# Second weight group of the first layer converted after the attention's scores, first group earlier

## The chip, the cores and the metric

The kernel runs on one core of one Trainium2 chip. Its time is device microseconds (us) of that core, from one launch with all inputs in device memory. Engines are named as in the profile: PE multiplies matrices (PEld is its loading of the stationary operand), DVE is the vector engine, ACT the scalar engine, POOL the GpSimd engine, SP the engine whose queue issues the DMAs. Each engine works through its own instructions in the order in which the program lists them, and waits on semaphores for what others make.

## The reference

```python
q_assign = argmax(norm(q) @ norm(centroids).T); k_assign likewise      # 2 x 8 heads, 768 tokens, 64 wide
scores = where(q_assign == k_assign, q @ k.T / sqrt(64), -1e9)
attn_out = softmax(scores) @ v
x  = attn_out as 1536 x 512
h  = x @ moe_w_in                       # 512 x 2048
x2 = (h * sigmoid(1.702 * h)) @ moe_w_out   # 2048 x 512
h2 = x2 @ moe2_w_in                     # 512 x 1024
out = layernorm(h2 * softmax(h2)) * g_ln @ moe2_w_out
```

Inputs are fp32. The weights `w_in` and `w_out` are read as pairs of 32-bit words (`raw`), turned into fp32 by integer operations, and split into two fp16 halves (high and low), so that each product is three fp16 matmuls.

## The kernel before

**Attention.** 16 heads in 8 pairs. A head has nine units (parts of its 768 x 768 scores), so there are 144 units, and units are also the clock by which due times are given. For each unit PE makes a first product whose row maxima DVE takes (line 927, then the reduction in line 938), then the scores (lines 982 and 983, a PSUM bank `st`), ACT takes the exponential (line 991), ACT or DVE casts it to fp16 (line 996, `ph`), POOL or DVE subtracts to get the low half (line 1000, "the rest"), and PE multiplies by the values (lines 1015, 1018, 1019, `av`). For some units, and for every odd one from unit 120 on, the exponential stays in its PSUM bank: then DVE makes the rest, and the bank is free for a later score only when that is done.

**First weights.** `w_in` (object `w1`) has 16 chunks of 128 x 512 in four groups. A chunk is loaded (line 183), then *narrowed* by three DVE operations (lines 194, 199, 203, all reading and writing `reg`), then squared with a row sum on ACT (line 213). When the four chunks of a group are squared, PE adds up the sums (`bound`, line 139, tile `tot` or `ex`), DVE makes a power of two of it (lines 145 to 153), and each chunk is split: high on ACT (line 234), low on DVE (line 237). A load needs a raw buffer (two in the attention, a third in the first layer), which comes free when an earlier chunk is narrowed. `w_out` (object `wo`) goes the same way, in one group of 16 chunks.

**First layer.** 48 steps of 12 matmuls (line 1187, tile `hps`), of which steps 1 to 8 need the first group, 9 to 16 the second, and so on to the fourth; the last 16 use all. Each step is followed by the gate (line 1194) and the high half (line 1197) on ACT, and by the low half on DVE (line 1205) or POOL (lines 1202, 1203). Then come `w_out`'s products (lines 1352 and 1364) and the second block.

**What sets the order.** Everything up to the 48 steps is a list of tasks with a cost per engine, a due time and the tasks that it waits for. `Plan.order` places them one after another: on each engine it takes, of the tasks that can start within 0.1 us of the earliest, the one with the smallest due time. The kernel is then written out in that order, so each engine's queue is fixed by it; the chip itself waits only for data and buffers. `tail=0` marks the tasks of the attention whose end opens the first layer's buffers. `weights(w, c, due)` adds the tasks of group c. With `begun=True` only loads, narrowing and squares are added (as `tail=0`), and `later` keeps the group for `scaled`, which adds bound, power, high and low when the first layer is set up, in `rest_of_layer`.

Before the change the first group is due over units 20 to 122, and the second group's loads, narrowing and squares over units 122 to 144; its bound and splits wait for the scores. Third and fourth group are added in `rest_of_layer`.

Of the kernel before, what the change touches and what calls it, by code (L numbers as in the profile page):

```python
# [21 lines left out]
def kernel(  # L22
# [29 lines left out]
    NH = B * H  # L52
# [16 lines left out]
    E1 = -10  # L69
    E2 = 0  # L70
    E3 = 0
    NG = 2
    WDUE = 0
    XDUE = 60
    VDUE = 3
# [22 lines left out]
    LN = 512.0  # L98
    WLATE = 6
    WAHEAD2 = 6  # L100
    W0, W1 = 20, 122

    const = ctx.enter_context(tc.tile_pool(name="const", bufs=1))
    wp = ctx.enter_context(tc.tile_pool(name="wp", bufs=1))
# [198 lines left out]
    w1 = Weight(0, w_in, "w1", reg1, group=w_in.shape[0] // P)  # L303
# [121 lines left out]
    NU = 9  # L425
# [247 lines left out]
    def late(x):  # L673

        return [T["PC", 0, 0, 1]] if x else []
# [112 lines left out]
    def bound(t, sums):  # L788

        t["tile"] = bank(t)  # L790
        power_sum(t["tile"], sums)
# [62 lines left out]

    narrows = []

    def weights(w, c, due, after=None, then=None, scores=(), begun=False):


        sums, parts = [], {}  # L860
        kw = dict(tail=2 if after else 0)
        n = CV + bool(scores)
        open_, kw = kw, dict(tail=0) if begun else kw
        chunks = range(c * w.group, (c + 1) * w.group)

        def step(i, k):
            if k == 0:
                parts[i] = w.narrow(i)
            next(parts[i])

        def powers(a):
            w.powers[c] = power_from(a["tile"][:, 0:w.group])
            if then:
                then()

        for i in chunks:
            d = due(i)
            prev = add(
                dict(SP=(0.47, 1.46)), d, lambda t, i=i: w.load(i),
                after=[narrows[-n] if len(narrows) >= n else None] + list(scores or late(True)), **kw  # L880
            )
            for k, x in enumerate((0.34, 0.6, 0.6)):
                prev = add(
                    dict(DVE=x), d + 3 + k, lambda t, i=i, k=k: step(i, k),
                    after=[prev] + (after if after and w is wo else []), shared=True, **kw
                )
            narrows.append(prev)
            sums.append(add(dict(ACT=0.61), d + 6, lambda t, i=i: w.square(i), after=[prev], **kw))
        kw = open_
        if begun:  # L890
            later.append((w, c, sums, powers, due))
            return
        scaled(w, c, sums, powers, due, after, kw)

    later = []

    def scaled(w, c, sums, powers, due, after, kw):
        chunks = range(c * w.group, (c + 1) * w.group)
        d = due(chunks[-1])
        a = add(  # L900
            dict(PE=0.1), NH * NU if after else d + 8, lambda t: bound(t, w.squares(c)), after=sums + (after or []),
            take="acc" if after else "ex", **kw
        )
        a = add(dict(DVE=0.9), NH * NU if after else d + 8, lambda t, a=a: powers(a), after=[a], frees=a, **kw)
        for i in chunks[0:WLATE if w is wo else w.group]:
            b = add(
                dict(ACT=0.61), d + 12, lambda t, i=i: w.high(i),
                after=[a, at("WL", w, i - 2)], **kw
            )
            T["WL", w, i] = add(dict(DVE=0.66), d + 13, lambda t, i=i: w.low(i), after=[b], shared=True, **kw)  # L910
# [352 lines left out]
    def rest_of_layer():  # L1263

        scores = [t for t in plan.tasks if t["tail"] == 0]
        result = [t for t in plan.tasks if t["tail"] <= 1]
        steps = blocks + [(2, m) for m in range(NF)]
        n0 = NH * NU + 100
        for x in later:
            scaled(*x[:4], lambda i: n0 - 70, scores, dict(tail=2))  # L1270
        for c in range(NG, w1.n // w1.group):
            weights(w1, c, lambda i: n0 + WAHEAD + 4 * i - w1.n, after=scores)
        weights(wo, 0, lambda i: n0 + WOD + 4 * i, after=result, then=even, scores=scores)
        for k, (n, m) in enumerate(steps):
            x, d = Hidden(n, m, k % 2), n0 + 2 * k
            a = add(
                dict(PE=1.92), d, lambda t, x=x: x.products(),
                after=[T["WL", w1, w1.ready(m) - 1]] + (result if n == 2 else scores), take="acc", tail=2,
            )
            T["HP", k] = a  # L1280
            b = add(
                dict(ACT=0.46), d, lambda t, x=x: x.gate(), after=[a] + [at("HL", k - 6)] * x.out,
                frees=a if x.out else None, tail=2,
            )
            c = add(dict(ACT=0.5), d, lambda t, x=x: x.high(), after=[b], tail=2)
            T["HL", k] = add(
                dict(POOL=1.45) if x.out else dict(DVE=0.5), d, lambda t, x=x: x.low(), after=[c],
                frees=None if x.out else a, tail=2,
            )
# [3 lines left out]
    peaks_of(0)  # L1293
    values()
    weights(w1, 0, lambda i: W0 + (W1 - W0) * i / w1.group)
    weights(w1, 1, lambda i: W1 + (NH * NU - W1) * (i - w1.group) / w1.group, begun=True)
    for p in range(NH // 2):
        if p:
            operands_of(p)
# [283 lines left out]
```

## Time and profile before

| | us |
|---|---|
| three runs | 618.36 median, 617.84 to 619.15 |
| the profiled execution | 617.67 |
| its span in the trace | 615.9 |
| PE busy in the span | 600.4 (97%) |
| DVE, ACT, POOL busy | 430.3, 391.9, 272.7 |

The profiled execution is 1.77 us longer than its span (the launch around it) and 0.69 us below the median of the three runs. In the profile a group or an instruction is named by engine, line, operation and tiles; behind an instruction stands in brackets how long its engine had been idle, and what ended that. Rows of windows give the busy time of each engine in a stretch, with the instruction count in brackets, and PEclk is the share of the full TensorE clock (2.4 GHz) that was granted.

### The profile page before, as it was taken

What the parts mean: (1) busy time and instruction counts of PE and PEld (TensorE: products, weight loads), DVE (VectorE), ACT (ScalarE), POOL (GpSimd) and SP (SyncE); (2) the same over time, 40 slices, a digit from 0 to 9 for tenths busy, and PEclk for the clock granted to TensorE, in tenths of its full rate; (3) what the DMA queues carried; (4) which work ended last, traced back from release to release, by engine and by line L of the source; (5) the groups of instructions that cost most, each with busy time, mean ns of one, the idle gap of its engine ahead of it and who ended that gap; (6) DMA issues with size and microseconds to landing.
All of it is one profiled execution on the core that took longest, in us unless ns stands there. A gap on an engine that the chain in (4) does not pass through costs nothing. (4 is left out here: it accounts for less than half of the span.)

```text
span 615.9 us, 12736 instructions
## 1 busy us (share of the span) xinstructions
PE 600.4 (97%) x4873; PEld 393.8 (64%) x4873; DVE 430.3 (70%) x967; ACT 391.9 (64%) x768; POOL 272.7 (44%) x247
## 2 busy tenths in 40 slices
PE   7999999999999979999999999999999999999997
PEld 6787788888788755666656666666665554444444
DVE  6999998899899997798985043075966455654542
ACT  4498899898899877878787055435335334544442
POOL 7259987776678762356643019600000112331320
PEclk9999999999999997999999999999999999999999
DMA  8898989968885156445630002051410112434241
GB/s 188 209 234 173 193 165 174 180 153 162 174 173 120 29 129 173 127 137 181 196 103 0 1 1 71 0 171 36 136 35 2 36 34 52 100 55 103 52 102 52
DMA packets 78772, 67.91 MB, mean 110 GB/s; under 512 B 61636, under 2 KB 64536, under 8 KB 78712
## 3 DMA queue, kind: packets, MB, share of 16 engines
q1 hardware_dynamic: 78712, 67.11, 46.2%
q8 instruction: 38, 0.62, 0.4%
q14 instruction: 22, 0.18, 0.1%
HBM read 34.64 MB, written 3.15 MB: 61 GB/s over the span
## 5 line engine op out<-in xcount | busy, mean ns | idle before, releaser
L1000 POOL TENSOR_TENSOR ph<-p,ph 128x512 f16<-128x512 f32 x108 | 129.9, 1219 | 53.7 <-ACT ph L996 27.9
L1187 PE MATMUL hps<-xT,reg 128*128 128x384 f16 x768 | 128.2, 330 | 0.0
L1187 PEld LDWEIGHTS <-reg 128*128 128x128 f16 x768 | 76.1, 100 | 50.7 <-issue 2.7
L938 DVE TENSOR_REDUCE nma<-sm 128x1 f32<-128x512 f32 (+1 forms) x144 | 96.6, 679 | 6.5 <-PE sm L927 5.8
L1364 PE MATMUL yps<-g,reg 128*128 128x384 f16 x576 | 94.6, 326 | 0.0
L1364 PEld LDWEIGHTS <-reg 128*128 128x128 f16 x576 | 56.4, 98 | 37.0
L1454 POOL TENSOR_TENSOR rs<-va,mhalf 128x1 f32<-128x1 f32 x12 | 6.6, 550 | 150.9 <-DVE va L1452 150.9
L1202 POOL TENSOR_SCALAR g<-g,scl 128x384 f32<-128x384 f32 x40 | 33.5, 838 | 88.8 <-ACT g L1197 81.2
L982 PE MATMUL st<-OP 128*128 128x256 f32 (+1 forms) x191 | 69.9, 377 | 2.5 <-DVE ph L1000 1.1
L991 ACT ACTIVATE p<-st 128x512 f32<-128x512 f32 x107 | 63.4, 597 | 9.2 <-PE st L983 8.2
L1413 PE MATMUL h<-reg,xT 128*128 128x512 f16 x288 | 64.1, 379 | 0.0
L1019 PE MATMUL av<-vh,ph 128*128 128x65 f16 x576 | 61.3, 195 | 1.7 <-POOL ph L1000 1.4
L983 PE MATMUL st<-OP 97*128 97x512 f32 (+3 forms) x191 | 62.8, 340 | 0.0
L1015 PE MATMUL av<-vh,ph 128*128 128x65 f16 x576 | 62.1, 194 | 0.0
L1018 PE MATMUL av<-vh,ph 128*128 128x64 f16 x576 | 61.4, 193 | 0.0
L1015 PEld LDWEIGHTS <-ph 128*128 128x128 f16 x576 | 52.7, 99 | 12.6 <-issue 11.2
L927 PE MATMUL sm<-OP 80*128 80x512 f32 x192 | 58.1, 359 | 1.1 <-DMA OP<-oht 0.7
L996 ACT CAST ph<-p 128x512 f16<-128x512 f32 x94 | 57.1, 616 | 1.2 <-PE av L1019 0.7
L1019 PEld LDWEIGHTS <-ph 128*128 128x128 f16 x576 | 53.6, 97 | 2.2 <-POOL ph L1000 1.9
L1018 PEld LDWEIGHTS <-ph 128*128 128x128 f16 x576 | 53.7, 97 | 0.1
L1489 PEld LDWEIGHTS <-g 128*128 128x128 f16 x312 | 30.4, 98 | 32.1 <-DMA g<-g 0.7
L1413 PEld LDWEIGHTS <-xT 128*128 128x128 f16 x288 | 28.2, 98 | 33.4
(204 smaller groups left out, 1132.7 us busy)
## 6 DMA issues: line engine op xcount, KB each, us to landing
OP<-hl SPq DMA_DIRECT2D x48, 384.0 KB, 4.8
raw<-in_moe_w_in_dram SPq DMA_DIRECT2D x24, 512.0 KB, 3.8
raw<-in_moe_w_out_dram SPq DMA_DIRECT2D x24, 512.0 KB, 3.4
xT<-in_v_dram SPq DMA_DIRECT2D x8, 384.0 KB, 4.5
out_dram<-ob SPq DMA_DIRECT2D x11, 256.0 KB, 2.3
raw<-in_k_dram SPq DMA_DIRECT2D x12, 192.0 KB
raw<-in_q_dram SPq DMA_DIRECT2D x12, 192.0 KB, 5.9
OP<-oht SPq DMA_DIRECT2D x30, 48.0 KB, 2.7
```

The lines of the kernel that those rows point to most:

```text
L927: nc.tensor.matmul(t["tile"][:, at], Q1[0:KM, j * P:(j + 1) * P], K1[0:KM, cs], start=True, stop=True)
L938: nc.vector.tensor_reduce(out=out, in_=src, op=ALU.max, axis=AX.X, negate=True)
L982: nc.tensor.matmul(t["tile"][:, at], K2[:, ks], Q2[:, cs], start=True, stop=False)
L983: nc.tensor.matmul(t["tile"][:, at], K1[0:n, ks], Q1[0:n, cs], start=False, stop=True)
L991: nc.scalar.activation(p32s[u, m], t["tile"], AF.Exp, scale=SCALE)
L1000: e.tensor_tensor(out=phs[u, m][:, 1], in0=p32s.pop((u, m)), in1=phs[u, m][:, 0], op=ALU.subtract)
L1015: nc.tensor.matmul(av[:, i, :], ph[:, 0, qs], vh[:, u, kt, D:], start=(m == 0 and i == 0), stop=False,)
L1018: nc.tensor.matmul(av[:, i, 0:D], ph[:, 0, qs], vh[:, u, kt, 0:D], start=False, stop=False)
L1019: nc.tensor.matmul(av[:, i, :], ph[:, 1, qs], vh[:, u, kt, D:], start=False, stop=(m == NU - 1 and kt == NJ - 1 and i == NJ - 1),)
L1187: nc.tensor.matmul(self.ps, w1.at(c, m, e), xT[:, x, c, n * TB:(n + 1) * TB], start=(c == 0 and e == x), stop=(c == ND - 1 and e == 1),)
L1364: nc.tensor.matmul(yps, wo.at(f, c, e), lp["g", n][:, x, f, :], start=(f == 0 and e == x), stop=(f == NF - 1 and e == 1),)
L1413: nc.tensor.matmul(h, xT[:, x, c, t * P:(t + 1) * P], w2.half(i * ND + c, e), start=(c == 0 and e == x), stop=(c == ND - 1 and x == 1),)
```

## The change

The first group's due times now run over units 20 to 80. The second group is no longer begun in the attention: all its tasks are added in `rest_of_layer`, like those of the third and the fourth, with due times behind the scores and its bound after them. `begun`, `later` and `scaled` go.

```diff
-    NG = 2
+    NG = 1
-    W0, W1 = 20, 122
+    W0, W1 = 20, 80
...
-    def weights(w, c, due, after=None, then=None, scores=(), begun=False):
+    def weights(w, c, due, after=None, then=None, scores=()):
...
         kw = dict(tail=2 if after else 0)
         n = CV + bool(scores)
-        open_, kw = kw, dict(tail=0) if begun else kw
...
-        kw = open_
-        if begun:
-            later.append((w, c, sums, powers, due))
-            return
-        scaled(w, c, sums, powers, due, after, kw)
...
-        for x in later:
-            scaled(*x[:4], lambda i: n0 - 70, scores, dict(tail=2))
         for c in range(NG, w1.n // w1.group):
             weights(w1, c, lambda i: n0 + WAHEAD + 4 * i - w1.n, after=scores)
...
     weights(w1, 0, lambda i: W0 + (W1 - W0) * i / w1.group)
-    weights(w1, 1, lambda i: W1 + (NH * NU - W1) * (i - w1.group) / w1.group, begun=True)
```

The plan reorders all engines. Lines of the changed kernel behind the removed ones are 12 to 15 lower (938 is 926, 991 is 979, 996 is 984, 1000 is 988, 1187 is 1175, 1205 is 1193).

DVE at the end of the attention, before: `ph` and `st` are the rests and casts of the last units, `reg1` with raw_3930 and raw_4415 the second group's second and third chunk.

```order
L1000 TENSOR_TENSOR ph_4461<-st_4385,ph_4461 128x512
L203 SCALAR_TENSOR_TENSOR reg1_105<-raw_3930,reg1_105 128x512
L1000 TENSOR_TENSOR ph_4478<-st_4427,ph_4478 128x512
L194 TENSOR_SCALAR reg1_105<-raw_4415 128x512
L1045 CAST xh_4528<-xs_4273 128x768
L199 SCALAR_TENSOR_TENSOR reg1_105<-raw_4415,reg1_105 128x512
L1030 TENSOR_SCALAR ri_4539<-av_4348 128x6
L1032 RECIPROCAL ri_4539<-ri_4539 128x6
L1000 TENSOR_TENSOR ph_4537<-st_4473,ph_4537 128x512
```

The same units now; raw_3240 is the second group's first chunk.

```order
L988 TENSOR_TENSOR ph_4431<-st_4385,ph_4431 128x512
L984 CAST ph_4468<-st_4428 128x512
L988 TENSOR_TENSOR ph_4468<-st_4428,ph_4468 128x512
L199 SCALAR_TENSOR_TENSOR reg1_105<-raw_3240,reg1_105 128x512
L988 TENSOR_TENSOR ph_4510<-st_4470,ph_4510 128x512
L1018 TENSOR_SCALAR ri_4538<-av_4348 128x6
L1020 RECIPROCAL ri_4538<-ri_4538 128x6
L203 SCALAR_TENSOR_TENSOR reg1_105<-raw_3240,reg1_105 128x512
```

Between the last reduction and the last rest DVE had ten narrowing operations (lines 194 to 203); it now has three, and one more stands earlier. The other eight of the second group come behind the last rest.

ACT at the same place, before: the third and the fourth square stand on either side of the last unit's exponential (`st_4594`).

```order
L991 ACTIVATE st_4582<-st_4582 128x512
L991 ACTIVATE p32_4599<-st_4588 128x512
L213 ACTIVATE junk_104,wss_101<-reg1_105 128x512
L991 ACTIVATE st_4594<-st_4594 128x512
L996 CAST ph_4637<-p32_4599 128x512
L213 ACTIVATE junk_104,wss_101<-reg1_105 128x512
```

And now:

```order
L984 CAST ph_4609<-p32_4568 128x512
L979 ACTIVATE p32_4618<-st_4580 128x512
L213 ACTIVATE junk_104,wss_101<-reg1_105 128x512
L979 ACTIVATE st_4613<-st_4613 128x512
L984 CAST ph_4651<-st_4613 128x512
L213 ACTIVATE junk_104,wss_101<-reg1_105 128x512 x2
L1182 ACT_TABLE_LOAD
```

One square, the group's first, stands ahead of the last exponential in place of three; the second and third follow the last cast, and the fourth comes in the first layer.

PE where the first layer begins, before: the last value matmuls, the second group's bound, the first step.

```order
L1019 LDWEIGHTS ph
L1019 MATMUL av<-vh,ph 128x65
L139 MATMUL tot<-wss,ones 128x4
L1187 LDWEIGHTS reg_105
L1187 MATMUL hps<-xT,reg_105 128x384
```

And now, where the first step begins (the last unit's twelve value matmuls follow it), and where the bound stands, behind the fifth step:

```order
L1007 LDWEIGHTS ph
L1007 MATMUL av<-vh,ph 128x65
L1175 LDWEIGHTS reg_105
L1175 MATMUL hps<-xT,reg_105 128x384
L1175 LDWEIGHTS reg_105
```

```order
L1175 LDWEIGHTS reg_105
L1175 MATMUL hps<-xT,reg_105 128x384
L139 MATMUL tot<-wss,ones 128x4
L1175 LDWEIGHTS reg_105
L1175 MATMUL hps<-xT,reg_105 128x384
```

The bounds of third group, fourth group and `w_out` stood behind steps 9, 16 and 39; they now stand behind steps 13, 21 and 44. The first group's bound, which stood among the attention's last third on PE, stands near its middle, and six casts of the attention's units have gone from DVE to ACT.

## Rows read from the trace of the kernel before

**Rows 1.** The page's first part: busy time, share, instructions.

```profile
PE 600.4 (97%) x4873; PEld 393.8 (64%) x4873; DVE 430.3 (70%) x967; ACT 391.9 (64%) x768; POOL 272.7 (44%) x247
```

**Rows 2.** Windows by stage: length, PE, PEld, DVE, ACT, POOL, PEclk, DMA, GB/s.

```profile
80.00:150.00 70.00, 70.00 (x901) 59.80 (x898) 63.67 (x133) 62.85 (x120) 52.53 (x44) 1.00 0.88 175
150.00:205.00 55.00, 54.19 (x723) 45.04 (x722) 49.60 (x106) 49.78 (x96) 42.58 (x35) 1.00 0.64 134
205.00:232.00 27.00, 21.51 (x343) 16.54 (x339) 25.98 (x45) 20.63 (x43) 15.53 (x13) 0.98 0.39 89
240.00:310.00 70.00, 70.00 (x435) 42.37 (x433) 61.97 (x113) 56.95 (x124) 36.99 (x35) 1.00 0.52 164
```

**Rows 3.** Waits from 205 to 233 us: in total, times, longest.

```profile
ACT junk L213 <- DVE reg L203: 5.3, 4, 3.1
...
PE tot L139 <- ACT junk L213: 1.6, 1, 1.6
PE av L1019 <- POOL ph L1000: 1.4, 2, 0.8
...
PE st L982 <- DVE ph L1000: 1.1, 2, 0.6
...
PE st L982 <- ACT p L991: 0.9, 1, 0.9
```

**Rows 4.** Timeline of DVE, ACT and PE at the attention's end.

```profile
218.44 1.66 DVE L203 SCALAR_TENSOR_TENSOR reg<-raw,reg 128x512 uint32<-128x512 uint32 x1
...
220.13 0.63 ACT L213 ACTIVATE junk<-reg 128x512 bf16<-128x512 f32 x1 [0.90 <-DVE reg L203]
...
220.76 0.58 ACT L991 ACTIVATE st<-st 128x512 f32<-128x512 f32 x1
...
222.41 0.38 PE L982 MATMUL st<-OP 128*128 128x256 f32 x1 [0.86 <-ACT p L991]
...
232.04 0.59 PE L139 MATMUL tot<-wss,ones 128*128 128x4 f32 x2 [1.59 <-ACT junk L213]
```

**Rows 5.** Groups of 205 to 232 us: count, busy, mean ns, idle before.

```profile
L203 DVE SCALAR_TENSOR_TENSOR reg<-raw,reg 128x512 uint32<-128x512 uint32 x4 | 5.2, 1294 | 0.0
...
L199 DVE SCALAR_TENSOR_TENSOR reg<-raw,reg 128x512 uint32<-128x512 uint32 x5 | 4.1, 824 | 0.0
...
L194 DVE TENSOR_SCALAR reg<-raw 128x512 uint32<-128x512 uint32 x5 | 2.7, 536 | 0.0
L213 ACT ACTIVATE junk<-reg 128x512 bf16<-128x512 f32 x4 | 2.5, 631 | 5.3 <-DVE reg L203 5.3
```

**Rows 6.** Windows of line 1187 on PE: length, PE, PEclk, DMA, GB/s.

```profile
230.00:235.00 5.00, 2.51 (x8) 0.58 0.36 107
235.00:240.00 5.00, 5.00 (x24) 0.74 0.98 217
240.00:245.00 5.00, 5.00 (x33) 1.00 0.57 175
```

**Rows 7.** Groups of 80 to 205 us on DVE.

```profile
L996 DVE CAST ph<-p 128x512 f16<-128x512 f32 x11 | 5.1, 468 | 0.8 <-ACT p L991 0.8
...
L199 DVE SCALAR_TENSOR_TENSOR reg<-raw,reg 128x512 uint32<-128x512 uint32 x4 | 3.9, 966 | 0.1
...
L237 DVE SCALAR_TENSOR_TENSOR reg<-reg,scl 128x512 f16<-128x512 f32 x4 | 3.1, 796 | 0.0
...
L203 DVE SCALAR_TENSOR_TENSOR reg<-raw,reg 128x512 uint32<-128x512 uint32 x4 | 2.9, 737 | 0.0
...
L194 DVE TENSOR_SCALAR reg<-raw 128x512 uint32<-128x512 uint32 x4 | 2.2, 556 | 0.0
```

**Rows 8.** Groups of 240 to 310 us on DVE.

```profile
L199 DVE SCALAR_TENSOR_TENSOR reg<-raw,reg 128x512 uint32<-128x512 uint32 x23 | 18.6, 816 | 0.1
L203 DVE SCALAR_TENSOR_TENSOR reg<-raw,reg 128x512 uint32<-128x512 uint32 x23 | 16.5, 722 | 0.1
...
L194 DVE TENSOR_SCALAR reg<-raw 128x512 uint32<-128x512 uint32 x22 | 13.2, 605 | 0.6 <-DMA raw<-in_moe_w_out_dram 0.6
...
L1205 DVE SCALAR_TENSOR_TENSOR g<-hps,scl,g 128x384 f16<-128x384 f32 x18 | 10.8, 609 | 5.9 <-ACT g L1197 5.9
```

**Rows 9.** Timeline of PE and DVE in the first layer.

```profile
252.53 0.28 PE L139 MATMUL tot<-wss,ones 128*128 128x4 f32 x2
252.67 13.81 PE L1187 MATMUL hps<-xT,reg 128*128 128x384 f16 x84
...
257.43 1.41 DVE L237 SCALAR_TENSOR_TENSOR reg<-reg,scl 128x512 f16<-128x512 f32 x2
```

More of the change, by code (lines that the diff above doesn't have):

```diff
@@ L888, in weights @@
             sums.append(add(dict(ACT=0.61), d + 6, lambda t, i=i: w.square(i), after=[prev], **kw))
-        kw = open_
-        if begun:
-            later.append((w, c, sums, powers, due))
-            return
-        scaled(w, c, sums, powers, due, after, kw)
[L895 to L899, printed above, removed]
         a = add(
```

## Prediction

> **What bounds the kernel now.** I read the busy times first. PE is busy for 97% of the span [rows 1], so any gain must come from the little time in which it stands still or runs slowly. Next I read the windows by stage, to see where that is. From 80 to 150 us PE has no idle at all, from 150 to 205 us it has 0.81 us, and in the first layer, from 240 to 310 us, none. But from 205 to 232 us, where the attention ends, PE is busy for 21.51 of 27 us, while DVE is busy for 25.98 [rows 2]. So in this one stretch DVE is the bound, and PE loses 5.49 us. Then I read the waits of that stretch: PE waits for scores' banks that DVE or ACT has not freed, for rests that POOL makes late, and 1.6 us in one piece for the second group's bound; ACT waits 5.3 us for narrowing [rows 3]. The groups say what fills DVE: narrowing, 2.7 + 4.1 + 5.2 us for 14 operations, most of them of the second group [rows 5]. The timeline shows how it hurts: a 1.66 us narrowing starts at 218.44, ACT stands idle for 0.90 us until it ends and squares, the exponential behind that square starts at 220.76, and 0.86 us of PE idle at 222.41 is put down to ACT's exponentials [rows 4]. Last, the windows of the first steps: the granted clock is 0.58 and 0.74 in the two windows from 230 to 240 us and full behind them [rows 6].
>
> **The change, part by part.**
>
> *End of the attention.* Of ten narrowing operations among the last rests, three stay. The seven that go are three of line 194, two of 199, two of 203: 3 x 0.536 + 2 x 0.824 + 2 x 1.294 = 5.8 us of DVE [rows 5]. DVE would then be busy for some 20 of the 27 us, less than PE's 21.51, so PE is the bound again and the most that can be won is its idle time, 5.49 us. Of this, 1.59 us is the wait at 232.04 for the second group's square [rows 4], and that bound now stands five steps later on PE, with the first step in its place. The other 3.9 us are not all narrowing: the 1.4 us that value matmuls waited for POOL [rows 3] have POOL's own length in them. I leave 1.2 us of idle, somewhat more than the 0.81 us of 150 to 205 us, which is a longer stretch. Gain 4.3 us; bounds 1.6 (only the bound's wait goes) and 5.5.
>
> *Clock.* A granted 0.58 over five us is 4.2 us at the low level of 1.2 GHz, and 0.74 is 2.6 us; if they are one piece it ends at 237.6. Matmuls run from 232.04 on [rows 4], so 5.6 us of them went at half rate, and 2.8 us were lost. What PE did ahead of it: it stood idle for pieces of up to 0.8 us, waiting for POOL's rests [rows 3], and then for 1.59 us. With the step in front of the bound, and with twelve value matmuls behind it, PE has work through the gap. I take the 2.8 us as won; bounds 0 and 2.8. The Trainium skill, "TensorE: Matmul & The Clock Gate", section "What's actually happening", says that the throttled clock is the default and activity releases it, by how busy PE has been recently. That agrees with the windows here, where the clock falls behind the idle pieces; by it the 2.8 us go with them, and by the opposite reading (the end of the attention drops the clock however it is filled) nothing goes, which is a rival below.
>
> *First group earlier.* The fourth chunk's narrowing and all four lows move from 150 to 205 us into 80 to 150 us: 0.556 + 0.966 + 0.737 + 4 x 0.796 = 5.4 us, and about 1 us for the bound's small operations; four casts leave DVE there, 4 x 0.468 = 1.9 us [rows 7]. So DVE gains 4.6 us of work in a stretch where it has 70 - 63.67 = 6.3 us free and PE none [rows 2]. It fits, but hardly, and PE can't make up there what it loses. I take 1.0 us lost. Bounds: a gain of 0.8 us, all the idle of 150 to 205 us, since that stretch is relieved, and a loss of 4.6 us, if nothing of the work fits in. SP's queue has the same loads earlier; I price that at nothing, because DVE was never idle ahead of the four operations of line 194, which use them [rows 7].
>
> *Second group in the first layer.* Eight narrowing operations are behind the last rest, against two before; that is two more of line 194, two of 199 and two of 203, which is 2 x (0.605 + 0.816 + 0.722) = 4.3 us [rows 8]. What is late next? First the bound behind step five. Its four squares need the eight operations, and two of the third group's stand among them: 3 of line 194, 4 of 199, 3 of 203, 3 x 0.605 + 4 x 0.816 + 3 x 0.722 = 7.2 us; between them stand a normalization, a cast, and a low of the first step, at most 0.61 us each [rows 8], and five small ones, some 1 us, so 10 us; the square takes 0.82 with its read-out. That is 10.8 us behind the last rest. PE needs (13.81 - 0.17)/84 = 0.162 us for a matmul [rows 9], 1.95 us for a step; five steps and twelve value matmuls are 10.2 us, and by the order its first step needs POOL's last rest, which I put about a us behind the start of DVE's. So PE comes to the bound at about 11 us, DVE and ACT at about 11: a draw. I take 0.6 us of waiting; bounds 0 and 2.3 (lines 203 and 199 as in the tail's worst group: 4 x 0.01 + 3 x 0.57 = 1.7, plus the 0.6). Then the splits: in the trace the last low of the third group ended at 258.84, 6.3 us behind its bound's start at 252.53 [rows 9]. Three steps are 5.9 us, and the fourth chunk is read in the last quarter of the ninth, 1.5 us later. I take 0.3 us; bounds 0 and 2. The third and the fourth group have eight steps, 15.6 us, from bound to bound, for four chunks that need 4 x 2.1 = 8.6 us of DVE. `w_out`'s bound is five steps, 9.8 us, later on PE and has 4.3 us more in front of it on DVE, which was free for 8 us from 240 to 310 us [rows 2]. I take 0.2 us, and in all 1.1 us lost.
>
> The sum against the profiled execution: 617.67 - 4.3 - 2.8 + 1.0 + 1.1 = 612.7 us. The median of the runs is 0.7 us above that execution, so the forecast is 618.36 - 5.0 = 613.4 us. Behind the first layer nothing moves: PE is full there, and it takes the gain along.
>
> **The rivals.** A measurement of this kernel can tell 0.2%, 1.2 us, from no change.
>
> First, the clock falls all the same. For it: idle pieces of 0.6 to 0.9 us stay possible ahead of the first step, where POOL makes the last rests. Against it: the longest piece goes. Then 2.8 us are not won: 616.2 us, still faster.
>
> Second, the attention's end is bound by the chain of exponential, cast and POOL rest, and not by DVE. For it: POOL's rests kept PE waiting for 1.4 us [rows 3]. Against it: DVE was busy for 96% of the stretch. Then only the bound's 1.6 us go, the clock falls, and the losses take 1 to 2 us of that: 618.0 to 618.9, no change.
>
> Third, slower: the first layer starves for the second group. The place is the bound behind step five. The price: if its narrowing meets POOL's lows as single operations did in the tail (1.66 us against a mean of 0.72 to 0.82), four of the seven long operations cost 3.5 us more, PE stands for 3.5 to 4 us in one piece, the clock falls there and costs the 2.8 us again, and the ninth step waits 1.2 us: 7.6 us lost, against 4.3 + 2.8 - 1.0 = 6.1 won. That is 619.9 us. It decides from the point on where the fourth chunk's last narrowing ends later than some 13 us behind the last rest. For it: DVE was busy for 61.97 of 70 us in the first layer [rows 2]. Against it: PE was busy for all 70 us there [rows 2].
>
> That the change does not do what it says is partly so: one and a third chunks of the second group still go ahead of the last rest, since its loads don't wait for the scores; the sum has them.
>
> **How the numbers follow.** The forecast has 0.56 (610.8 to 615.3 as its own range: all idle of the tail won and no loss, or 2 us more lost), the first rival 0.16, the second 0.14, the slower one 0.14. So faster is 0.72, the same 0.14, slower 0.14. The range goes from 610.8 to 618.6: it leaves out the slower case and little below.
>
> **What would show it.** Right: from 205 us to the first step PE idles about 1.5 us instead of 5.5, DVE is no longer full there, ACT's wait for narrowing is below 1.5 us, the first steps of line 1175 come 1.95 us apart at full clock, and line 139 behind step five waits for less than 1 us. Wrong: PE idle between 80 and 150 us of more than 2 us, a wait of line 139 or of the ninth step of more than 2 us, or a low clock behind either.

## The result and the profile after

The changed kernel took 610.59 us (median of 4 runs, 609.75 to 611.14) beside 618.1 us for the kernel before on the same chip: ratio 0.988, 95% interval 0.9854 to 0.9906. In a second set it took 611.12 us (6 runs, 610.21 to 613.57) beside 617.62 us: 0.9904, interval 0.9886 to 0.9923. So it is faster, clear of the noise, by 6.5 to 7.5 us or a little over 1%; 5.0 us were forecast. The profiled execution took 611.14 us with a span of 609.3 us, 6.5 us less than before.

The busy times of the changed kernel, to be held against [rows 1]: PE's busy time is 3.3 us shorter for the same 4873 instructions, which full clock in place of the low one explains for the most part (2.5 us, as worked out in the part on the prediction), and its share is a point higher.

```profile
PE 597.1 (98%) x4873; PEld 393.1 (65%) x4873; DVE 429.1 (70%) x962; ACT 393.8 (65%) x773; POOL 269.5 (44%) x247
```

The windows by stage of the changed kernel, which answer to [rows 2] (length, PE, PEld, DVE, ACT, POOL, PEclk, DMA, GB/s):

```profile
80.00:150.00 70.00, 69.45 (x882) 57.90 (x878) 64.32 (x135) 64.44 (x125) 48.37 (x41) 1.00 0.86 180
150.00:205.00 55.00, 54.54 (x735) 46.45 (x734) 48.85 (x98) 50.58 (x96) 41.61 (x36) 1.00 0.69 132
205.00:232.00 27.00, 25.98 (x390) 20.68 (x389) 23.60 (x47) 22.94 (x45) 16.90 (x15) 1.00 0.36 79
232.00:240.00 8.00, 6.82 (x44) 4.02 (x42) 5.87 (x14) 5.79 (x13) 2.81 (x4) 1.00 0.91 181
240.00:310.00 70.00, 70.00 (x435) 42.39 (x434) 63.14 (x112) 57.58 (x123) 37.86 (x35) 1.00 0.50 160
```

From 205 to 232 us PE is now busy for 25.98 instead of 21.51 us, and DVE for 23.60 instead of 25.98. But the first step now starts at 226.61 us, so this window holds 5 us of the first layer. The 27 us that end where PE turned to the first layer compare like with like; first the kernel before, up to the bound in front of its first step, then the changed kernel:

```profile
205.04:232.04 27.00, 21.47 (x342) 16.50 (x338) 25.98 (x45) 20.59 (x43) 15.50 (x12) 0.98 0.39 89
199.61:226.61 27.00, 25.98 (x425) 22.04 (x425) 23.97 (x45) 24.54 (x47) 20.64 (x17) 1.00 0.29 52
```

There too DVE falls below PE: it was busy for 96% of the stretch and is for 89%, and PE, with 96%, is the bound. From 80 to 150 us PE idles 0.55 us that it did not before; from 150 to 205 us it idles 0.46 instead of 0.81. New is an idle of 1.18 us from 232 to 240.

The groups of 205 to 232 us in the changed kernel, against [rows 5] (count, busy, mean ns, idle before):

```profile
L199 DVE SCALAR_TENSOR_TENSOR reg<-raw,reg 128x512 uint32<-128x512 uint32 x3 | 2.6, 853 | 0.0
...
L203 DVE SCALAR_TENSOR_TENSOR reg<-raw,reg 128x512 uint32<-128x512 uint32 x3 | 2.0, 677 | 0.0
L213 ACT ACTIVATE junk<-reg 128x512 bf16<-128x512 f32 x3 | 1.9, 630 | 3.0 <-DVE reg L203 3.0
...
L194 DVE TENSOR_SCALAR reg<-raw 128x512 uint32<-128x512 uint32 x2 | 0.8, 419 | 0.0
```

Eight narrowing operations for 5.4 us, where fourteen took 12.0. Line 203 is not only rarer: its mean fell from 1294 to 677 ns. Two of its three now run behind the last rest, while POOL stands still (the last section comes back to this).

The first steps of the first layer on PE, windows of line 1175 (1187 before), against [rows 6]:

```profile
230.00:235.00 5.00, 5.00 (x33) 3.00 (x31) 1.00 1.10 240
235.00:240.00 5.00, 3.57 (x23) 2.06 (x22) 1.00 0.74 188
240.00:245.00 5.00, 5.00 (x33) 2.99 (x32) 1.00 0.35 131
```

The granted clock is 1.00 throughout, where it was 0.58 and 0.74. The first step starts at 226.61 us instead of 232.49, and the second has the usual 1.95 us.

What is left of the waits from 205 to 240 us, against [rows 3] (in total, times, longest):

```profile
ACT junk L213 <- DVE reg L203: 4.7, 3, 2.3
...
PE tot L139 <- ACT junk L213: 1.2, 1, 1.2
PE av L1007 <- POOL ph L988: 1.0, 2, 0.7
DVE reg L194 <- DMA raw<-in_moe_w_in_dram: 0.9, 1, 0.9
```

PE no longer waits for scores' banks. ACT still waits for narrowing, but for squares that stand behind the last exponential (224.30 us), which hold up no score. The 1.2 us wait is that of the second group's bound behind step five. The timeline of DVE, ACT and PE shows what it waits for:

```profile
232.49 0.62 DVE L1193 SCALAR_TENSOR_TENSOR g<-hps,scl,g 128x384 f16<-128x384 f32 x1 [1.74 <-ACT g L1185]
233.03 0.42 DVE L194 TENSOR_SCALAR reg<-raw 128x512 uint32<-128x512 uint32 x1
234.31 0.43 DVE L194 TENSOR_SCALAR reg<-raw 128x512 uint32<-128x512 uint32 x1 [0.87 <-DMA raw<-in_moe_w_in_dram]
234.66 2.01 DVE L199 SCALAR_TENSOR_TENSOR reg<-raw,reg 128x512 uint32<-128x512 uint32 x2
...
237.30 0.63 ACT L213 ACTIVATE junk<-reg 128x512 bf16<-128x512 f32 x1 [1.74 <-DVE reg L203]
...
238.07 0.39 PE L139 MATMUL tot<-wss,ones 128*128 128x4 f32 x2 [1.18 <-ACT junk L213]
```

At 233.03 DVE begins the second group's last chunk. The next in its queue, at 234.31, is the third group's first chunk, whose load has not landed: DVE stands for 0.87 us with the last chunk half done, and the square comes at 237.30. Ahead of the chunk DVE had stood for 1.74 us more, in front of the first step's low half, which waits for ACT.

### The profile page after: what moved, and what is told of

It reads as the page before. It is cut to its first block, busy times and chain, and to the rows that moved or that the text cites. A ratio compares the mean times of both kernels' runs of the same rounds, so it can differ in the third digit from the quotient of the medians.

```text
span 609.3 us, 12749 instructions
## 1 busy us (share of the span) xinstructions
PE 597.1 (98%) x4873; PEld 393.1 (65%) x4873; DVE 429.1 (70%) x962; ACT 393.8 (65%) x773; POOL 269.5 (44%) x247
## 5 line engine op out<-in xcount | busy, mean ns | idle before, releaser
L988 POOL TENSOR_TENSOR ph<-p,ph 128x512 f16<-128x512 f32 x108 | 126.3, 1187 | 57.0 <-ACT ph L984 29.9
L1175 PE MATMUL hps<-xT,reg 128*128 128x384 f16 x768 | 126.0, 326 | 0.0
L1003 PEld LDWEIGHTS <-ph 128*128 128x128 f16 x576 | 52.7, 99 | 12.2 <-issue 10.7
L984 ACT CAST ph<-p 128x512 f16<-128x512 f32 x99 | 60.1, 619 | 0.3
```

The lines of the kernel that those rows point to most:

```text
L984: e(phs[u, m][:, 0], p32s[u, m])
L988: e.tensor_tensor(out=phs[u, m][:, 1], in0=p32s.pop((u, m)), in1=phs[u, m][:, 0], op=ALU.subtract)
L1003: nc.tensor.matmul(av[:, i, :], ph[:, 0, qs], vh[:, u, kt, D:], start=(m == 0 and i == 0), stop=False,)
L1175: nc.tensor.matmul(self.ps, w1.at(c, m, e), xT[:, x, c, n * TB:(n + 1) * TB], start=(c == 0 and e == x), stop=(c == ND - 1 and e == 1),)
```

## The experiments

The theory was that two things cost the kernel before its 5.5 us at the attention's end and the low clock behind it: DVE, filled by narrowing, and the bound that stood in front of the first step. What the early first group does was open. I took the change apart first (E1, E2), then its two suspects (E3, E4).

**E1, the deferral alone.** The changed kernel with the first group as late as before:

```diff
-    W0, W1 = 20, 80
+    W0, W1 = 20, 122
```

> The second group waits as in the changed kernel, but the first group keeps its due times over units 20 to 122. Theory A (the gain comes from the attention's end and from the handoff; where the first group converts is worth nothing): 610.6 us within 1.0, PE idle from 80 to 150 us near 0 again and that of 150 to 205 us near 0.8. Theory B (the early first group relieves the last third of the attention and is part of the gain): 613 us or more.

Measured: 613.13 us, ratio 0.9935 (0.9911 to 0.9959) to 617.85 us. From 205 us to the first step PE idled 1.1 us, as in the full change, and the first step started at 225.61 us, earlier than there, though with 36 value matmuls still behind it where the full change has 12. The loss is in the first layer. Waits, `w_out`'s bound, and windows of line 1175:

```profile
PE tot L139 <- ACT junk L213: 2.6, 1, 2.6
```

```profile
318.74 0.40 PE L139 MATMUL tot<-wss,ones 128*128 128x16 f32 x2 [1.05 <-ACT junk L213]
```

```profile
235.00:240.00 5.00, 2.11 (x14) 1.18 (x12) 1.00 0.49 91
240.00:245.00 5.00, 5.00 (x23) 2.57 (x21) 0.66 0.70 231
```

The bound behind step five waited 2.6 us, the clock fell to 0.66 behind it, and the next two steps took 3.30 and 2.28 us instead of 1.95. A third loss is 1.05 us of waiting at `w_out`'s bound (318.74 us). That is the course of the slower rival, a long wait there with a low clock behind it, in half its size. The profiled execution is the longest of the four (614.9 us): in two of them the mean clock over the span was 1.00, and they took 612.21 and 612.66 us, so the fall of the clock does not come every time, and 1 to 2 us are lost to the changed kernel without it too. Why it waited longer than in the full change stands in the timelines. The deferral alone, DVE and SP's queue:

```profile
225.78 1.57 DVE L203 SCALAR_TENSOR_TENSOR reg<-raw,reg 128x512 uint32<-128x512 uint32 x1
```

```profile
227.38 3.19 SPq L183 DMA_DIRECT2D raw<-in_moe_w_in_dram  x3
```

and the changed kernel:

```profile
220.50 0.65 DVE L203 SCALAR_TENSOR_TENSOR reg<-raw,reg 128x512 uint32<-128x512 uint32 x1
```

```profile
221.18 7.48 SPq L183 DMA_DIRECT2D raw<-in_moe_w_in_dram  x3
```

The operation of line 203 is the last on the second group's first chunk. When it ends, its load buffer is free and the next loads are issued: at 227.38 us here, at 221.18 us there. That this lateness makes the wait is a reading of the two timelines so far; E7, E12 and E13 test it.

**E2, the early first group alone.** The kernel before, in which only the first group's due times end at unit 80:

```diff
-    weights(w1, 0, lambda i: W0 + (W1 - W0) * i / w1.group)
+    weights(w1, 0, lambda i: W0 + (80 - W0) * i / w1.group)
```

> The first group goes over units 20 to 80, but the second group is still begun in the attention over units 122 to 144, with its bound ahead of the first step. Theory A: 617 to 619 us, PE idle at the attention's end still over 4 us and the clock falling behind it. Theory B: 613 to 615 us.

Measured: 613.82 us, ratio 0.9946 (0.9927 to 0.9966). PE's idle time from 205 us to the first step fell from 5.5 to 3.55 us, but the clock fell as before; windows by stage, and of line 1187:

```profile
205.00:232.00 27.00, 23.45 (x361) 18.25 (x362) 23.86 (x51) 22.23 (x47) 14.57 (x12) 0.92 0.43 100
```

```profile
225.00:230.00 5.00, 0.96 (x4) 0.66 (x5) 0.77 0.46 140
230.00:235.00 5.00, 5.00 (x19) 2.44 (x18) 0.55 0.19 70
```

The bound in front of the first step now runs at 228.60 us, so the window from 205 us holds 3.4 us of what follows it. The 27 us up to the bound are these, against 25.98 us of DVE and 21.47 us of PE in the kernel before:

```profile
201.60:228.60 27.00, 23.44 (x389) 19.29 (x387) 24.57 (x44) 23.79 (x49) 17.97 (x15) 0.98 0.41 89
```

So the first group's earlier place emptied the attention's end too, though less than the full change: DVE lost 1.4 us there, with eleven narrowing operations for 8.1 us in place of fourteen for 12.0. Each half of the change alone is thus worth 4.0 to 4.7 us by medians. (The profiled execution of E2 is the longest of its four, 615.01 us, so its trace shows only 2.7 of the 4.0.) The two sum to 8.7 us, more than the whole, since both take idle time out of the same stretch.

**E3 and E4, the squares and the bound.** Both are the kernel before with the second group's bound due after the first steps; the order put it behind five. In E3 the group's squares also wait for the scores:

```diff
+            if begun:
+                sums.append((prev, i))
+                continue
...
-            scaled(*x[:4], lambda i: n0 - 70, scores, dict(tail=2))
+            x[2][:] = [
+                add(dict(ACT=0.61), n0 - 75, lambda t, i=i, w=x[0]: w.square(i), after=[p] + scores, tail=2)
+                for p, i in x[2]
+            ]
+            scaled(*x[:4], lambda i: n0 - 70, scores, dict(tail=2), n0 + 9)
```

> The kernel before, with the second group's four squares on ACT behind the scores and its bound due behind five steps; the narrowing on DVE stays among the last rests. Theory A1 (DVE's own load makes PE idle at the attention's end): within 1 us of the kernel that only moves the bound, about 613.5 us, and over 3 us of PE idle stay ahead of the first step. Theory A2 (it is ACT standing in front of the squares, with the exponentials queued behind them): about 611 us, and PE idle ahead of the first step falls to some 1.5 us.

E4 has the bound's new due time alone (in both, `scaled` takes it as a new argument; that part is left out here):

```diff
-            scaled(*x[:4], lambda i: n0 - 70, scores, dict(tail=2))
+            scaled(*x[:4], lambda i: n0 - 70, scores, dict(tail=2), n0 + 9)
```

> The kernel before, with one due time changed: the second group's bound comes behind five steps of the first layer in place of ahead of the first; all engines' order in the attention is as before. Theory A (the long wait at the bound is what drops the clock): the 1.6 us wait and 2.5 us of half-rate steps go, 614.0 us, clock 1.0. Rival (the clock falls for the shorter pieces of idle ahead of it, or because the attention ends there): only 1.6 us go, 616.5 us, and the first two steps take 3.8 and 2.6 us as before.

Measured: E3 613.91 us, 0.9944 (0.9928 to 0.9961); E4 614.8 us, 0.9954 (0.9937 to 0.9971). PE idled 2.9 us ahead of the first step in E3 and 4.0 us in E4, so the squares in front of exponentials cost 1.1 us, and the larger part stays with DVE, busy for 26.29 us in E4 (26.59 in E3). That is nearer the first of the two theories. Yet in E4 the clock does not fall; windows by stage, and of line 1187:

```profile
205.00:232.00 27.00, 23.02 (x345) 17.36 (x345) 26.29 (x46) 20.19 (x42) 15.52 (x12) 1.00 0.38 92
```

```profile
230.00:235.00 5.00, 5.00 (x32) 3.03 (x31) 1.00 0.53 162
```

The idle pieces ahead of the first step are those of the kernel before without the last, of 1.59 us. So the clock fell for that wait: with work in its place it holds. It was not the full length of the wait that did it, as the kernel before shows; the wait there runs from 230.45 to 232.04 us (length, PE, PEclk, DMA, GB/s):

```profile
230.00:230.70 0.70, 0.45 (x15) 1.00 0.00 0
230.80:232.04 1.24, 0.00 (x0) 0.50 0.00 0
```

The clock was at the low level 0.3 us into the wait. By the mean clock of each execution it held in five of seven of E4 (0.999 or 1.00) and not in two (0.997), and it fell in all ten of the kernel before in that set (0.994 to 0.997). Part of the gain came back: the third group's bound waits 1.5 us behind step eight.

**E9, the early first group and the bound behind two steps.** E2 with the second group's bound due at `n0 + 3`, nine of its narrowing operations still among the last rests.

> The kernel before with the first group over units 20 to 80, the second group still begun in the attention (this much alone measured 613.8 us), and in addition the second group's bound planned behind two steps of the first layer instead of in front of them. The narrowing stays among the last rests, nine operations of it. If the wait at the bound with the slow clock behind it is what this kernel lost (2 us of wait of ACT's squares, steps of 3.79 and 2.79 us), it goes and the time is 609.5 to 611 us, equal to the full change without deferring any narrowing. If DVE's fullness among the last rests is what counts, as my prediction had it, PE still idles 2.5 to 3.5 us from 205 us to the first step, and the time is 611.5 to 612.5 us. A fall of the clock in spite of the moved bound would leave 613 us or more.

Measured: 612.15 us, 0.991 (0.9897 to 0.9923) to 617.62 us. Windows by stage:

```profile
205.00:232.00 27.00, 24.37 (x378) 19.32 (x377) 24.07 (x46) 22.33 (x47) 16.14 (x14) 1.00 0.42 95
```

The clock stays at 1.00, and PE idles 2.6 us there: the second of the cases that I had written down. In the full change it is 1.02 us. So with the clock saved, narrowing among the last rests still costs PE some 1.6 us of idle: that is what deferring it takes away. In time E9 is 1.0 us above the changed kernel of the same set (611.12 us); each has a wait at a bound in the first layer besides, of 0.8 us at the third group's in E9.

**E6 and E7, chunks in order.** The changed kernel (E6) and the deferral alone (E7), with this edit to the narrowing's predecessors, so that the third group's first chunk can't stand in the middle of the second group's last:

```diff
-                    after=[prev] + (after if after and w is wo else []), shared=True, **kw
+                    after=[prev] + (after if after and w is wo else []) + (narrows[-1:] if w is w1 and c > 1 else []), shared=True, **kw
```

> The changed kernel, in which a chunk of the third and fourth group is narrowed only behind the chunk before it in the plan; the bound of the second group comes out behind six steps instead of five. My theory: the 1.2 us wait at the bound is there because the third group's first chunk stands on DVE in the middle of the second group's last chunk, and waits 0.9 us for its load there. Then the wait goes: the first steps come 1.95 us apart without the 3.54 us one, and the time is 1.2 us below the changed kernel, about 609.4 us. Rival: DVE has too much work there whatever the order (eight operations of the second group behind the last rest); then the wait only moves, to the third group's bound or to the ninth step, and the time is within 0.4 us of the changed kernel.

> The deferral alone (first group over units 20 to 122, as in the kernel before; measured 613.1 us) with the same edit: the third group's first chunk behind the second group's last. The deferral alone waited 2.6 us at the bound behind step five, and the next three steps took 3.30 us and less before they were 1.95 again, so its clock fell. My theory: the first group's earlier place is worth 2.5 us beside the deferral because it lets the second group's chunk be narrowed sooner, and so shortens this wait to one that keeps the clock. Then an order that shortens the wait by another means gives much of the same: wait of 1 to 1.7 us, no fall of the clock, 610.6 to 611.8 us. Rival: the first group's place is worth 2.5 us by something in the attention, which this edit doesn't touch: 612.7 to 613.3 us.

E6 took 610.56 us, 0.9883 (0.9865 to 0.99), beside 611.12 us for the changed kernel in the same set. PE idled nowhere from 232 to 310 us, but its waits up to 330 us have new ones:

```profile
PE yps L1337 <- issue: 1.5, 1, 1.5
PE tot L139 <- ACT junk L213: 1.2, 1, 1.2
```

The wait moved from the second group's bound to that of `w_out`, now at 317.65 us behind step 46, with only two steps left to cover what follows it: the rival. The edit held back every chunk, not one. The profiled execution is the longest of E6's five (611.95 us); the shortest took 608.76 us, and no trace tells whether it had these waits. In E7 it did not touch the wait, which stayed at 2.6 us: the second group's last chunk itself was late there. The time was 612.58 us, 0.9915 (0.9903 to 0.9927), and the run tells nothing on the theory.

> The changed kernel once more, unedited, as the measure for the three kernels beside it and for the scatter between executions. Its runs so far have a median of 610.6 us and its profiled execution took 611.1 us, 6.5 us less than the profiled execution of the kernel before, while the medians differ by 7.5 us. If the one microsecond between these is scatter of single executions, the new profiled execution lies anywhere from 609.8 to 611.2 us with the same steps: first step at about 226.6 us, 1.2 us of wait at the bound behind step five, products of w_out from about 322.7 us. If it is a part of the gain that I have not found, the trace shows the same stages and the median stays 7.5 us below the kernel before.

The changed kernel, run again in that set, had the same stages (first step at 226.0 us, a wait of 1.3 us, products of `w_out` from 322.15 us). Its profiled execution took 610.58 us and its median was 611.12 us, 6.5 us under the kernel before: of the 7.5 us of the first set about one was scatter, or scatter hides one here.

**E10, one chunk in order.** The same edit for the third group's first chunk alone. In the order that the plan makes of it, the second group's bound comes behind step six in place of five, and `w_out`'s behind step 45:

```diff
-                    after=[prev] + (after if after and w is wo else []), shared=True, **kw
+                    after=[prev] + (after if after and w is wo else [])
+                    + (narrows[-1:] if w is w1 and i == 2 * w.group else []), shared=True, **kw
```

> The changed kernel with the narrowing of one chunk alone, the third group's first, put behind the second group's last (the run before put all chunks of the third and fourth group in order, and the 1.2 us wait moved from the second group's bound to w_out's, behind step 46, with 1.5 us more ahead of the products of w_out). Here w_out's bound is planned behind step 45, one later than in the changed kernel. If the wait moved because every chunk was held back, it is gone here at both places: 609.4 us. If the order of one chunk is enough to push all later loads back, the wait stands at w_out's bound again, 0.5 to 1.2 us, and the time is within 0.4 us of the changed kernel.

Measured: 608.47 us (607.99 to 608.56), 0.9861 (0.9848 to 0.9874) to 616.76 us. Windows by stage:

```profile
205.00:232.00 27.00, 25.98 (x391) 20.47 (x390) 23.12 (x47) 23.05 (x44) 16.50 (x14) 1.00 0.45 88
232.00:240.00 8.00, 8.00 (x52) 4.94 (x51) 6.42 (x17) 6.71 (x14) 4.43 (x5) 1.00 0.61 165
```

The 1.18 us of 232 to 240 are gone and came back nowhere. Two things moved, the last square and the bound:

```profile
235.34 0.63 ACT L213 ACTIVATE junk<-reg 128x512 bf16<-128x512 f32 x1
...
237.80 0.28 PE L139 MATMUL tot<-wss,ones 128*128 128x4 f32 x2
```

The square starts 9.6 us behind the first step (225.73 us), against 10.7 us in the changed kernel (237.30 behind 226.61). Behind five steps PE would have come at about 236.0 us, by the 10.3 us that it needed in the changed kernel, and the square's sum was read out by 236.1: so, by this estimate, the order of the chunk took away nearly all of the wait, and the sixth step in front only the rest.

The span is 606.7 us, 2.6 below the changed kernel's first and 2.1 below its second. Of this, 1.4 to 1.5 us lie between the first step and the first product of `w_out` (94.66 us against 96.09 and 96.15), where the edit acts. Another 0.3 to 0.9 us lie ahead of the first step, where DVE, ACT and POOL have the same order up to 225 us: that is scatter, and not the edit's. It is the fastest version of the case; by the ratios to the kernel before it beats the changed kernel clearly in the second set (0.9886 to 0.9923) and with overlapping intervals in the first. The two were not timed on one chip.

**E12 and E13, the second group's first chunk early.** The deferral alone (E12) and the changed kernel (E13), with that chunk's narrowing not held back for POOL's work in the plan; it stands ahead of the last reduction then:

```diff
-                    after=[prev] + (after if after and w is wo else []), shared=True, **kw
+                    after=[prev] + (after if after and w is wo else []),
+                    shared=not (after and w is w1 and i == w.group), **kw
```

> The deferral alone (first group over units 20 to 122, measured 613.1 us), with one more edit in the plan: the narrowing of the second group's first chunk is not held back for GpSimd's work, so it stands ahead of the last reduction, four operations of the second chunk stand among the last rests, five come behind, and the bound is planned behind two steps. In the deferral alone the chunk's last narrowing ended at 227.3 us, and only then the third chunk's load was issued (227.38 us; in the changed kernel 221.18 us). My theory: this buffer, freed late, is what costs the deferral alone its 2.6 us wait and the low clock behind it, and the first group's earlier place is worth 2.5 us only because it frees it sooner. Then this kernel, whose first group is as late as before, waits less than 1.3 us in the first layer, keeps the clock at 1.0 and takes 610 to 611.5 us. Rival: the first group's place counts in the attention itself, or DVE has too much work behind the scores anyway: the wait stays at 2 us or more, 612.5 to 613.5 us.

> The changed kernel (610.6 and 611.1 us in two sets of runs) with the same edit: the second group's first chunk is narrowed whole ahead of the last reduction, three operations of its second chunk stand among the last rests as in the changed kernel, five instead of eight come behind the last rest, and the bound is planned behind two steps. If my theory holds that the 1.2 us wait at the bound is only the lateness of the second group's last chunk, the wait goes, nothing is left but some 1.0 us of idle from 205 us to the first step, and the time is 1 to 1.5 us below the changed kernel (609.4 to 610 us). Rival, as in the run with the chunks in order: PE's time in the first layer is set by the last of all loads and narrowings, and a wait taken away at one bound comes back at a later one or at the products of w_out: within 0.5 us of the changed kernel.

E12 took 613.61 us, 0.994 (0.9926 to 0.9954), and E13 610.78 us, 0.9902 (0.9888 to 0.9917). In both the wait at the second group's bound is gone, though the bound stands three steps earlier; it was 2.6 us in E1 and 1.2 us in the changed kernel. What is left is 0.4 us at the third group's bound. So the wait does follow from when that chunk is narrowed; whether by its buffer or by the three operations fewer that are left behind the last rest, these two runs don't separate. But the time did not follow. Windows of E12:

```profile
150.00:205.00 55.00, 52.40 (x672) 43.26 (x671) 49.91 (x103) 47.56 (x90) 40.30 (x33) 0.98 0.66 136
```

and of E13:

```profile
150.00:205.00 55.00, 53.61 (x726) 45.67 (x723) 49.98 (x99) 49.78 (x96) 43.28 (x36) 1.00 0.67 141
```

PE idles 2.60 us from 150 to 205 us in E12, with a clock of 0.98, and 1.39 us in E13, against 0.46 in the changed kernel and 0.81 and 1.32 in the kernel before [rows 2] and in E1: one chunk more in that stretch costs 0.9 us where the first group has left it, and more where it has not. What was won at the bound was paid there. My expectation for E12 missed: I had the wait right, and its rival had the time. With the clock at 1.00 throughout, as in two of its six executions, it took 611.61 and 612.42 us, so a part of what it paid is the clock's fall. E13 is within 0.5 us of the changed kernel, as its rival said, though the loss stands in the attention and not at a later bound.

## Why the prediction fell short of the gain

The direction and the places were right, the size was 1.5 to 2.5 us too small. The lower end of the range was also added up wrongly: all idle of the tail won and no loss is 618.36 - 5.5 - 2.8 = 610.1 us, and not 610.8. By its steps, in the profiled executions:

- *End of the attention*, priced at 4.3: from 205 to 232 us PE's idle fell from 5.49 to 1.02 us, 4.5 us. DVE was the bound there and no longer is; I had it at some 20 of 27 us, and it is 23.97 in the 27 us ahead of the first step, since the denser stretch has more of the attention's own work in it (nine reductions, where there were three). E9 and E4 show both parts, DVE's load and the bound. One sign was off: ACT's wait for narrowing stayed at 3.0 us where I had below 1.5, but no exponential stands behind it any more.
- *Clock*, priced at 2.8: the first two steps took 3.79 and 2.60 us before, against 1.95 at full clock, so 2.5 us. E4 shows that it needed the 1.59 us wait. With the idle gone the clock stays at 1.00, so the rival by which it falls anyway is refuted. The Trainium skill, "TensorE: Matmul & The Clock Gate", section "What's actually happening", says that the clock is set by how busy PE has been recently. These traces agree with that.
- *First group earlier*, priced at a loss of 1.0: **this is the step that failed.** "It fits, but hardly, and PE can't make up there what it loses": PE did lose 0.55 us from 80 to 150 us, but 150 to 205 us gave 0.35 back, so 0.2 us were lost. And I priced the step as if it ended there. E2 shows that alone it is a gain of 4.0 us: it empties DVE at the attention's end by 1.4 us (24.57 against 25.98 in 27 us) even with the second group in place. Beside the deferral (E1 against the full change) it is worth 2.0 to 2.5 us by medians: the second group's first chunk is narrowed 6 us earlier, which frees its load buffer sooner, and it is done without filling the stretch of 150 to 205 us beyond what it holds, as E12 did. (How much of that is the buffer is not shown: E12 narrows the chunk early too, but leaves less behind the last rest as well.) Without it the next step would have cost 2.6 us of wait, a low clock in some executions, and 1.05 us at `w_out`'s bound, as in E1. I had counted its loads at nothing.
- *Second group in the first layer*, priced at a loss of 1.1: 1.18 us, all at the bound behind step five; I had 0.6 there, 0.3 at the ninth step and 0.2 for `w_out`, which waited for nothing, so that the sum agrees is luck. The cause was one that I had in the sum only as two operations of the third group: they brought a late load with them into the queue (E10). The sum also lacks the 1.74 us in which DVE stood in front of the first step's low half.

These come to 4.5 + 2.5 - 0.2 - 1.2 = 5.6 us of the 6.5 by which the profiled executions differ. The other 0.9 us are not PE's idle: over the whole span that fell by 3.3 us (615.9 - 600.4 against 609.3 - 597.1), and the idle in this list comes to 3.1. They are in PE's busy time, by my count 0.7 of them ahead of the first step, and what shortened it no run shows. The first set's medians differ by another microsecond, which the second set does not repeat.

Of the rivals, the second (a chain of exponential, cast and POOL bounds the end) fell: with DVE relieved, 1.0 us of waiting for POOL is all that is left there. The slower one did not come about in the changed kernel but did in E1, at its place and with its fall of the clock, for 2.6 + 1.7 us, and 1.05 at `w_out`'s bound, instead of 7.6. There it began with the second group's first chunk, narrowed late, and not with POOL's lows, as the rival had it.

## What to carry to other kernels

A step that is moved earlier frees more than its own time: follow what its buffer lets in, and what that lets in further on, before it is priced as a mere displacement. A queue that runs in order is only as early as the latest load of any instruction in it, so an operation whose input is late belongs behind the one that something waits for; here one such swap (E10), with the bound one step later, won the 1.2 us that the change had left there. And a wait taken away at one place is won only if the windows up to the next full stretch show that it stands nowhere else.

## What the runs showed of the hardware

Neither the sum of PE's idle time nor the length of one wait settled the clock. In E4 PE idled 4.0 us ahead of the first step in pieces of at most 0.9 us, and the clock stayed at 1.00. In the kernel before the same pieces were followed by a wait of 1.59 us, and the clock was low 0.3 us after that had begun. In E2 it was low from 227.75 us on, behind pieces of 0.61 and 1.21 us and at the start of one of 0.92 (0.77 and 0.55 in the windows). A wait of 1.2 us left it at 1.00 in the changed kernel and in E9; one of 2.6 us was followed by 0.66, but the low level came 0.8 us after PE had begun again (E1). And one kernel does not do the same each time: E1 lost clock in two of four executions, the changed kernel in one of ten (0.997).

Operations of lines 199 and 203 on DVE, all of one shape, took longer only beside POOL. In the trace of the kernel before there are 96; the 49 that ran while POOL stood still took 0.69 us at most, and each of the 20 that took more than 0.75 us ran beside an operation of POOL for over 0.5 us. Not every meeting lengthens one. Among the last rests of the kernel before, this is such a pair:

```profile
218.39 1.16 POOL L1000 TENSOR_TENSOR ph<-p,ph 128x512 f16<-128x512 f32 x1 [0.17 <-ACT ph L996]
218.44 1.66 DVE L203 SCALAR_TENSOR_TENSOR reg<-raw,reg 128x512 uint32<-128x512 uint32 x1
```

In the changed kernel POOL stands still from 226.23 to 230.84 us, and two of line 203 run there:

```profile
230.84 1.64 POOL L1037 TENSOR_TENSOR xh<-xs,xh 128x768 f16<-128x768 f32 x1 [4.61 <-DVE xh L1033]
```

```profile
227.15 0.69 DVE L203 SCALAR_TENSOR_TENSOR reg<-raw,reg 128x512 uint32<-128x512 uint32 x1
...
228.47 0.69 DVE L203 SCALAR_TENSOR_TENSOR reg<-raw,reg 128x512 uint32<-128x512 uint32 x1
```

So the fall of line 203's mean from 1294 to 677 ns goes with where the operations stand. No run moved POOL's operations alone.
